# Blockwise decaying attention and a Mish MLP on one core: the head in a new order, and the first two groups' states taken head by head

## The chip, the cores and the metric

The kernel runs on one core of a Trainium2 chip. The metric is the device time of one execution in microseconds (us). The engines are TensorE (PE in the profile, PEld for its weight loads), VectorE (DVE), ScalarE (ACT), GpSimd (POOL) and the queue of SyncE (SP). They run their own instruction streams in order and wait for each other by semaphores.

## What is computed

The reference runs a linear attention with a decay per head over blocks of 64 positions, and then a two-layer MLP on the result:

```python
for b in range(nb):                       # 12 blocks of 64; B, H, S, D = 4, 8, 768, 64
    intra = einsum('bhic,bhjc->bhij', qb, kb) * Dmask      # lam ** (i - j), causal
    intra = einsum('bhij,bhjd->bhid', intra, vb)
    inter = einsum('bhid,bhde->bhie', qb * lam_pow, kv_state)
    out[:, :, sl] = intra + inter
    kv_state = lam_block * kv_state + einsum('bhsd,bhse->bhde', kb * rev_pow, vb)
x = out as (3072, 512)
h = x @ w_in                              # w_in 512 x 2048
g = h * tanh(softplus(h))                 # Mish
result = g @ w_out                        # w_out 2048 x 512
```

## The kernel before

It works in chunks of 128 positions of one batch with all eight heads. Chunk c belongs to group c // 4 (six groups: positions 128 n to 128 n + 127 of the four batches). Heads are paired: JP = 4 pairs j, and t = 0, 1 within a pair.

For the chunks 0 to 7, the first two groups, three steps each do the attention on TensorE: `first_t` (the turn) transposes k and q (8 matmuls into the PSUM tiles `pk` and `pq`; ACT copies the first to `pkT`, DVE the second to `pqT`); `first_s` makes the scores (8 matmuls into two tiles `pS`, then two DVE products `sb` with the decay mask `dm` in group 0 and with a causal mask in group 1); `first_o` makes the outputs (8 matmuls with the values `vz` into `pO`, in group 1 also 4 with the state `wst`; ACT copies `pO` to `xt`, the MLP's input). `vz` is 128 wide for each head, with zeros in its upper half.

The first layer of the MLP for group 0 is 16 units u of four 128x512 matmuls (`mm1_unit`, L399), each followed by Mish on ACT; for group 1 it is 16 tiles of sixteen 128x128 matmuls (`mm1_tile`, L417). Before the last chunk of group 0 is there, `mm1_part` runs units 0, 1 and 2 on the first three chunks (384 columns), and the rest of 128 columns, the tail, follows. The second layer is `mm2_unit` (L431), four 128x512 matmuls each.

The states: `state_step` multiplies a chunk's decayed keys `ktil` (k times `lk`; made by `scale_k`, on DVE for group 0 and on POOL for group 1) with its values, in four 128x128 matmuls per chunk, one for each pair. That gives a pair's two own 64x64 blocks and two cross blocks. In group 0 a product with `lbm` (the block decay in the own blocks, zero elsewhere) writes `wst`. In group 1 the sum with `wst` goes to `raw`, and POOL writes the own blocks times the decay to `wcp`, in two 64x256 products per chunk. From group 2 on `group_state` does without cross blocks: sixteen matmuls for two chunks in 128x64 column tiles (L319), the lower 64 columns for t = 0 and the upper for t = 1.

From group 2 on, `turn` transposes by DMA on SP's queue (`qraw`, `kraw`), `pair_s` makes the scores of two chunks, `pair_o` their outputs, and these stand among the dense units of the group before. The loop of group 2's attention (n = NT - 1 = 1) runs among 32 `mm2_unit`, four for each chunk of groups 0 and 1: `pair_s` after units 9 and 16, `pair_o` after 13 and 20.

What sets the order: everything is written out by hand (`manual_schedule`), so each engine runs in program order. `busy(m)` puts m matmuls of zeros on TensorE. Loads of k, q, v and the weights go through POOL's queue in the order of the code, and `scale_k` of group 1 stands among them. A load that follows eight others waits until the one of the same semaphore has landed. PSUM has 8 banks: `ph` 2, `po` 2, `pS`, `pk`, `pq`, `pO` 1 each.

Of the kernel before, what the change touches and what calls it, by code (L numbers as in the profile page):

```python
# [20 lines left out]
def kernel(  # L21
# [12 lines left out]
    C = 128  # L34
# [117 lines left out]
    nc.vector.memset(one1, 1.0)  # L152
    for i in range(B):
        nc.vector.memset(vz[i][:, :, D : 2 * D], 0.0)
# [13 lines left out]
    busy(3)  # L168

    lnb = const.tile([128, H], F32, name="lnb")  # L170
    nc.scalar.activation(lnb, lamb, AF.Ln)

    dm = const.tile([128, 2, JP, C], F32, name="dm")
    lk = const.tile([128, H], F32, name="lk")
    lnp = const.tile([128, JP], F32, name="lnp")
# [10 lines left out]
    def pair_decays():  # L186
        lnh = lnb.rearrange("p (j t) -> p j t", t=2)
        for hp in range(2):
            rs = slice(64 * hp, 64 * hp + 64)
            nc.vector.tensor_copy(lnp[rs, :], lnh[rs, :, hp])  # L190

    def q_arguments():
        nc.vector.tensor_tensor(out=lq, in0=bc(ei, 1, JP), in1=bc(lnp, 2, C), op=ALU.mult)

    def q_decays():
        nc.scalar.activation(lq, lq, AF.Exp)
# [12 lines left out]
    def first_t(c):  # L209

        out_ = []
        first = c < B
        for src, name in ((k0 if c == 0 else kn[c] if first else ktil[c], "pk"),
                          (q0 if c == 0 else qn[c], "pq")):
            pt = ps.tile([128, JP, C], F16, name=name, tag=name)
            for j in range(JP):
                nc.tensor.matmul(
                    pt[:, j, :], src[:, 2 * j : 2 * j + 2, :].rearrange("p h c -> p (h c)"), ident,
                    is_transpose=True, start=(j == 0), stop=(j == JP - 1),
                )  # L220
# [23 lines left out]
    def first_o(c):  # L244
# [5 lines left out]
        for j in range(JP):  # L250
            if n:
                nc.tensor.matmul(psO[:, j, :], wst[b][j // 2][:, j % 2, :],
                                 kq[c][1][:, j, :], start=True, stop=False)
            for t in range(2):
                o = 4 * D * j + D * t
                nc.tensor.matmul(psO[:, j, :], vf[:, o : o + 128], sb0[c][t][:, j, :],
                                 start=(n == 0 and t == 0), stop=(t == 1))
# [20 lines left out]
    wst = [[const.tile([128, 2, 128], F16, name=f"w{b}{hf}") for hf in range(2)] for b in range(B)]  # L278
# [5 lines left out]
    def state_step(n, b, spare):  # L284

        i = n * B + b
        pv = ps.tile([128, JP, 128], F32, name="pv", tag=spare, bufs=2)
        for j in range(JP):
            nc.tensor.matmul(
                pv[:, j, :].rearrange("p (a e) -> p a e", a=2),  # L290
                ktil[i][:, 2 * j : 2 * j + 2, :].rearrange("p h c -> p (h c)"),
                vz[i % NVB][:, 2 * j : 2 * j + 2, 0:D], start=True, stop=True,
            )
        if n:
            raw = work.tile([128, JP, 128], F32, name="raw", tag="raw", bufs=4)
        for hf in range(2):
            hs = slice(2 * hf, 2 * hf + 2)
            if n == 0:
                nc.vector.tensor_tensor(
                    out=wst[b][hf], in0=pv[:, hs, :], in1=lbm[:, hs, :], op=ALU.mult)  # L300
            else:
                nc.vector.tensor_tensor(
                    out=raw[:, hs, :], in0=pv[:, hs, :], in1=wst[b][hf], op=ALU.add)
        if n:
            for t in range(2):
                rs = slice(64 * t, 64 * t + 64)
                nc.gpsimd.tensor_tensor(
                    out=wcp[b // 2][0][rs, b % 2, :, :], in0=raw[rs, :, rs],
                    in1=bc(lbc[rs, :], 2, D), op=ALU.mult)

    def group_state(n, spare):

        for h in range(2):
            pv = ps.tile([128, 2, JP, D], F32, name="pv", tag=spare, bufs=2)
            for x in range(2):
                i = n * B + 2 * h + x
                for j in range(JP):
                    for t in range(2):
                        nc.tensor.matmul(  # L319
                            pv[64 * t : 64 * t + 64, x, j, :], ktil[i][:, 2 * j + t, :],  # L320
                            vz[i % NVB][:, 2 * j + t, 0:D], start=True, stop=True)
            raw = work.tile([128, 2, JP, D], F32, name="raws", tag="raws", bufs=2)
            nc.vector.tensor_tensor(out=raw, in0=pv, in1=wcp[h][n % 2], op=ALU.add)  # L323
            nc.gpsimd.tensor_tensor(  # L324
                out=wcp[h][(n + 1) % 2], in0=raw, in1=bc(bc(lbc, 1, 2), 3, D), op=ALU.mult)

    def pair_a(s):
        if s.n < NG - 1:
            group_state(s.n, s.spare)
# [63 lines left out]
    def mm1_part(n, ni, lo, hi):  # L393

        if lo == 0:
            ph_t[ni] = ps.tile([128, GT], F32, name="ph",
                               tag="po" if n == 0 and ni == 2 else "ph", bufs=2)
# [85 lines left out]
    nc.scalar.preload_act_table(AF.Mish)  # L483
# [12 lines left out]
    first_s(3)  # L496
# [3 lines left out]
    mm1_part(0, 2, 0, GT - C)  # L500
    scale_k(0)
    nc.vector.memset(lbm, 0.0)
    for hp in range(2):
        rs = slice(64 * hp, 64 * hp + 64)
        nc.vector.tensor_copy(lbm[rs, :, rs], bc(lbc[rs, :], 2, D))
    for i in range(B, NVB - 2):
# [7 lines left out]
    load_q(NVB - 1)  # L514
    load_v(NVB - 1)
    scale_k(B + 2)
# [23 lines left out]
    for f, i in ((load_k, c + 1), (load_q, c + 1), (load_k, c + 2), (load_q, c + 2)):  # L540
        f(i)
    steps = {(4, 0): ((first_o, 5), (first_s, 6)), (4, 1): ((first_t, 7), (state_step, 0)),
             (4, 2): ((first_o, 6), (first_s, 7), (state_step, 1)), (4, 3): ((state_step, 2),),
             (5, 0): ((first_o, 7), (state_step, 3))}
    for c in range(B, 2 * B):
        for s in range(WS):
            mm1_tile(c, s)
            for f, i in steps.get((c, s), ()):
                f(*((1, i, "po") if f is state_step else (i,)))
# [5 lines left out]
    for n in range(NT - 1, NG):  # L555
# [9 lines left out]
        if n + 1 < NG:  # L565
# [5 lines left out]
            steps = (((9, pair_s, 0), (13, pair_o, 0), (16, pair_s, 1), (20, pair_o, 1),  # L571
# [60 lines left out]
```

## Time and profile before

| what | us |
|---|---|
| runs shown (3) | 211.38, 212.17, 212.15; median 212.15 |
| profiled execution, its time | 213.28 |
| its span, first to last instruction | 211.5 |
| TensorE busy / DVE / ACT / POOL | 203.1 / 69.3 / 86.3 / 102.4 |
| ACT's first Mish of group 0 starts | 19.71 |
| first matmul of the second layer | 54.91 |
| last matmul ends, about | 208.4 |

The time is the span and 1.8 us around it. In the profile a row of the timeline has the start, the time from the first start to the last end, the engine, the line, the operation, output <- inputs with their shapes, and in brackets the idle time of the engine before it with what ended that. Rows of the chain of waits have a start, a duration and a name. The state of the DMA engines matters here too: their mean busy share is 90% or more in each of the first 21 of the page's 40 slices.

### The profile page before, as it was taken

The numbers are of one execution on the slowest core, as the hardware profiler recorded it, in microseconds if no ns is written. First come the engines' busy times: TensorE is split into PE (matmuls) and PEld (weight loads), VectorE is DVE, ScalarE is ACT, GpSimd is POOL, SyncE is SP. The second block draws the span as 40 slices with busy tenths as digits, with TensorE's granted clock in tenths as the row PEclk, the third lists the DMA queues.
The fourth block names the chain that finished last, engine by engine and source line by source line (L and its number), as shares of the span: only waits on it lengthen the run. The fifth ranks groups of instructions, "written<-read, shape, count | busy, mean of one in ns | idle before, by whom it ended". The sixth has DMA issues, their size and how long they took to land.

```text
span 211.5 us, 4241 instructions
## 1 busy us (share of the span) xinstructions
PE 203.1 (96%) x1728; PEld 110.2 (52%) x1728; DVE 69.3 (33%) x131; ACT 86.3 (41%) x146; POOL 102.4 (48%) x149
## 2 busy tenths in 40 slices
PE   7798999999997999999999999999999999999994
PEld 2465546999644544455544454544445544444442
DVE  6867746650004442042440042582042600000000
ACT  5664566656321111356412356312456221566120
POOL 7997379948992558796965076931000000000000
PEclk9999999999999999999999999999999999999999
DMA  9999999999999999999996999996902032100112
GB/s 132 132 159 172 192 145 115 152 195 168 114 146 209 195 179 177 171 188 148 149 161 152 190 81 84 144 167 152 183 1 51 3 99 99 51 3 0 50 50 99
DMA packets 109894, 26.76 MB, mean 127 GB/s; under 512 B 102578, under 2 KB 106930, under 8 KB 109874
## 3 DMA queue, kind: packets, MB, share of 16 engines
q0 software_dynamic: 78080, 13.37, 91.8%
q1 hardware_dynamic: 27296, 6.63, 20.4%
q10 hardware_dynamic: 4498, 6.49, 9.9%
q8 instruction: 13, 0.21, 0.5%
q14 instruction: 7, 0.06, 0.1%
HBM read 27.26 MB, written 6.29 MB: 159 GB/s over the span
## 4 chain that ended last, share of the span: by engine, by line
PE 75%; POOL 13%; DMA 9%; issue 1%; DVE 0%; POOLq 0%
PE po L431 35%; PE ph L399 27%; DMA kn<-in_k_dram 6%; PE ph L417 5%; DMA kraw<-ktil 3%; POOL vz L79 3%; POOL ktil L266 3%; POOL qn L76 2%; POOL kn L68 2%; PE pS L343 2%; PE pO L370 2%; POOL win L92 1%; POOL win L95 1%; PE pv L319 1%; PE pO L349 1%
## 5 line engine op out<-in xcount | busy, mean ns | idle before, releaser
L431 PE MATMUL po<-wout,hsg 128*128 128x512 f16 (+2 forms) x400 | 85.4, 371 | 0.0
L399 PE MATMUL ph<-xt,win 128*128 128x512 f16 (+2 forms) x332 | 73.5, 371 | 0.4 <-ACT hsg L406 0.2
L406 ACT ACTIVATE hsg<-ph 128x512 f16<-128x512 f32 x80 | 47.5, 597 | 30.2 <-PE ph L399 29.8
L431 PEld LDWEIGHTS <-hsg 128*128 128x128 f16 x400 | 37.8, 98 | 42.3
L399 PEld LDWEIGHTS <-win 128*128 128x128 f16 x332 | 30.9, 98 | 34.7 <-issue 1.5
L446 ACT ACTIVATE osb<-po 128x512 f32<-128x512 f32 (+1 forms) x24 | 14.2, 593 | 75.4 <-PE po L431 70.6
L358 DVE TENSOR_TENSOR sb<-pS,maskT 128x512 f16<-128x512 f32 x32 | 20.0, 683 | 64.0 <-PE pS L343 64.0
L68 POOL DMA_DIRECT2D kn<-in_k_dram x23 | 20.9, 909 | 5.3 <-issue 1.9
L79 POOL DMA_DIRECT2D vz<-in_v_dram x24 | 21.6, 905 | 2.7 <-DMA win<-in_moe_w_in_dram 2.0
L76 POOL DMA_DIRECT2D qn<-in_q_dram x23 | 20.8, 903 | 3.3 <-DMA wout<-in_moe_w_out_dram 1.9
L266 POOL TENSOR_TENSOR ktil<-kn,lk 128x512 f16<-128x512 f16 x16 | 16.6, 1050 | 3.0 <-ACT hsg L406 2.9
L376 DVE TENSOR_TENSOR xtok<-pO,lqt 128x512 f16<-128x512 f32 x16 | 10.3, 686 | 16.8 <-PE pO L370 16.8
L417 PE MATMUL ph<-xt,win 128*128 128x128 f16 x256 | 15.3, 219 | 0.0
L417 PEld LDWEIGHTS <-win 128*128 128x128 f16 x256 | 14.5, 98 | 0.1
L440 DVE COPY osb<-po 128x128 f32<-128x128 f32 x1 | 0.3, 290 | 38.7 <-PE po L431 38.7
L421 ACT ACTIVATE hsg<-ph 128x512 f16<-128x512 f32 x16 | 9.6, 597 | 6.9 <-PE ph L417 6.9
L387 POOL COPY tick<-hsg 1x1 f16<-1x1 f16 x25 | 4.4, 176 | 12.2 <-ACT hsg L406 12.1
L324 POOL TENSOR_TENSOR wc<-raws,lbc 128x512 f16<-128x512 f32 x6 | 6.6, 1113 | 5.5 <-DVE raws L323 5.5
L163 PE MATMUL busy<-kzero 128*128 128x512 f16 x18 | 7.6, 516 | 1.2 <-DVE kzero L149 1.2
L266 DVE TENSOR_TENSOR ktil<-kn,lk 128x512 f16<-128x512 f16 (+1 forms) x8 | 6.6, 846 | 0.0
L241 DVE TENSOR_TENSOR sb<-pS,maskT 128x512 f16<-128x512 f32 x8 | 5.2, 686 | 4.2 <-PE pS L237 4.2
L343 PE MATMUL pS<-qraw,kraw 64*128 64x128 f16 x128 | 5.1, 218 | 1.2 <-DMA kraw<-ktil 1.2
(72 smaller groups left out, 122.6 us busy)
## 6 DMA issues: line engine op xcount, KB each, us to landing
out_dram<-osb ACTq DMA_DIRECT2D x23, 256.0 KB, 2.6
vz<-in_v_dram POOLq DMA_DIRECT2D x24, 128.0 KB, 4.7
kn<-in_k_dram POOLq DMA_DIRECT2D x23, 128.0 KB, 5.2
qn<-in_q_dram POOLq DMA_DIRECT2D x23, 128.0 KB, 5.0
wout<-in_moe_w_out_dram POOLq DMA_DIRECT2D x4, 512.0 KB, 10.4
win<-in_moe_w_in_dram POOLq DMA_DIRECT2D x3, 512.0 KB, 10.2
kn<-in_k_dram SPq DMA_DIRECT2D x1, 256.0 KB, 3.2
qn<-in_q_dram ACTq DMA_DIRECT2D x1, 256.0 KB, 3.9
```

The source lines that it names most:

```text
L68: nc.gpsimd.dma_start(out=kn[i], in_=chunk_rows(k, i))
L76: nc.gpsimd.dma_start(out=qn[i], in_=chunk_rows(q, i))
L79: nc.gpsimd.dma_start(out=vz[i % NVB][:, :, 0:D], in_=chunk_rows(v, i))
L266: (nc.vector if i < B or i >= (NG - 1) * B else nc.gpsimd).tensor_tensor(out=t, in0=kn[i], in1=bc(lk, 2, D), op=ALU.mult)
L358: nc.vector.tensor_tensor(out=s.sb[x][t], in0=pS[x][t], in1=bc(maskT, 1, JP), op=ALU.mult)
L376: nc.vector.tensor_tensor(out=xtok[:, :, :, t, :], in0=s.pO[t], in1=bc(bc(lqj[:, :, t], 1, 2), 3, D), op=ALU.mult)
L399: nc.tensor.matmul(ph_t[ni][:, lo:hi], win_t(ni, kc), xt[n][:, kc, lo:hi], start=(kc == 0), stop=(kc == NKC - 1))
L406: nc.scalar.activation(hsg[n][:, ni, :], ph_t.pop(ni), AF.Mish)
L417: nc.tensor.matmul(ph[:, u, :], win_t(w * s + u, kc), xt[n][:, kc, b * C : (b + 1) * C], start=(kc == 0), stop=(kc == NKC - 1),)
L421: nc.scalar.activation(hsg[n][:, w * s : w * s + w, b * C : (b + 1) * C], ph, AF.Mish)
L431: nc.tensor.matmul(po[:, lo:hi], hsg[n][:, ki, b * C : (b + 1) * C], wout[part][:, kk, lo:hi], start=(ki == 0), stop=(ki == NKI - 1),)
L446: nc.scalar.activation(o, i, AF.Copy)
```

## The change

The head (group 0's attention) is laid out anew, the decays by pair come from ScalarE, and the states of groups 0 and 1 are made head by head. Cut to what is spoken of:

```diff
+    half = const.tile([1, 2, 128], F32, name="half")
+    nc.vector.memset(half, 0.0)
+    for t in range(2):
+        nc.vector.memset(half[:, t, 64 * t : 64 * t + 64], 1.0)
...
     nc.tensor.matmul(lamb, one1, lam1, start=True, stop=True)
-    busy(3)
+    lamp = ps.tile([128, JP], F32, name="lamp", tag="pS")
+    for t in range(2):
+        nc.tensor.matmul(lamp, half[:, t, :], lam1.rearrange("p (j t) -> p j t", t=2)[:, :, t],
+                         start=(t == 0), stop=(t == 1))
+    busy(1)
...
-    def q_arguments():
-        nc.vector.tensor_tensor(out=lq, in0=bc(ei, 1, JP), in1=bc(lnp, 2, C), op=ALU.mult)
     def q_decays():
-        nc.scalar.activation(lq, lq, AF.Exp)
-        nc.scalar.activation(lqt, lnb, AF.Exp, scale=eq)
-    lbm = const.tile([128, JP, 128], F32, name="lbm")
+        for j in range(JP):
+            nc.scalar.activation(lq[:, j, :], ei, AF.Exp, scale=lnp[:, j : j + 1])
...
-    def first_t(c):
+    def first_t(c, m=0):
...
                 nc.scalar.activation(out_[-1], pt, AF.Copy)
+                busy(m)
...
+    def state_half(n, h, spare, bufs=2):
+        pv = ps.tile([128, 2, JP, D], F32, name="pv", tag=spare, bufs=bufs)
+        for x in range(2):
+            i = n * B + 2 * h + x
+            for j in range(JP):
+                for t in range(2):
+                    nc.tensor.matmul(
+                        pv[64 * t : 64 * t + 64, x, j, :], ktil[i][:, 2 * j + t, :],
+                        vz[i % NVB][:, 2 * j + t, 0:D], start=True, stop=True)
+        rows = [slice(64 * t, 64 * t + 64) for t in range(2)]
+        own = [wst[rs, 2 * h : 2 * h + 2, :, rs] for rs in rows]
+        if n == 0:
+            for rs, o in zip(rows, own):
+                nc.vector.tensor_tensor(
+                    out=o, in0=pv[rs], in1=bc(bc(lbc[rs, :], 1, 2), 3, D), op=ALU.mult)
+            return
+        raw = work.tile([128, 2, JP, D], F32, name="raws", tag="raws", bufs=2)
+        if n == 1:
+            for rs, o in zip(rows, own):
+                nc.vector.tensor_tensor(out=raw[rs], in0=pv[rs], in1=o, op=ALU.add)
+        else:
+            nc.vector.tensor_tensor(out=raw, in0=pv, in1=wcp[h][n % 2], op=ALU.add)
+        nc.gpsimd.tensor_tensor(
+            out=wcp[h][(n + 1) % 2], in0=raw, in1=bc(bc(lbc, 1, 2), 3, D), op=ALU.mult)
...
+    def clear(b):
+        nc.vector.memset(wst[:, b], 0.0)
+
     nc.scalar.activation(k0, kn[0], AF.Copy)
+    nc.scalar.activation(lnp, lamp, AF.Ln)
     decays(0)
-    pair_decays()
+    decays(1)
     nc.vector.tensor_copy(q0, qn[0])
     nc.scalar.activation(dm[:, 0], dm[:, 0], AF.Exp)
-    decays(1)
-    first_t(0)
+    first_t(0, 2)
+    clear(0)
     nc.scalar.activation(dm[:, 1], dm[:, 1], AF.Exp)
-    q_arguments()
+    nc.scalar.activation(lk, lnb, AF.Exp, scale=ek)
+    nc.scalar.activation(lqt, lnb, AF.Exp, scale=eq)
+    nc.scalar.activation(lbc, lnp, AF.Exp, scale=float(C))
     busy(1)
     first_s(0)
-    nc.scalar.activation(lk, lnb, AF.Exp, scale=ek)
-    nc.scalar.activation(lbc, lnp, AF.Exp, scale=float(C))
+    first_t(1)
+    clear(1)
     q_decays()
-    busy(2)
-    first_t(1)
-    nc.scalar.preload_act_table(AF.Mish)
     busy(1)
+    first_o(0)
     first_s(1)
-    first_o(0)
     busy(3)
     first_t(2)
-    busy(1)
+    clear(2)
+    nc.scalar.preload_act_table(AF.Mish)
+    first_o(1)
     first_s(2)
-    first_o(1)
     busy(3)
     first_t(3)
+    clear(3)
+    first_s(3)
     first_o(2)
-    busy(1)
-    first_s(3)
+    busy(2)
     mm1_part(0, 0, 0, GT - C)
     first_o(3)
     mm1_part(0, 1, 0, GT - C)
-    mm1_part(0, 2, 0, GT - C)
     scale_k(0)
-    nc.vector.memset(lbm, 0.0)
-    for hp in range(2):
-        rs = slice(64 * hp, 64 * hp + 64)
-        nc.vector.tensor_copy(lbm[rs, :, rs], bc(lbc[rs, :], 2, D))
+    scale_k(1)
...
+    scale_k(B + 2)
     load_v(NVB - 1)
-    scale_k(B + 2)
...
-    steps = {11: ((first_t, 4),), 13: ((first_s, 4),), 14: ((first_t, 5),),
-             15: ((first_o, 4), (first_s, 5), (first_t, 6))}
+    steps = {12: ((first_t, 4),), 14: ((first_s, 4),), 15: ((first_t, 5), (first_o, 4))}
     for u in range(NKI):
         mm1_unit(0, u)
-        if u in (3, 5, 7, 9):
-            state_step(0, (u - 3) // 2, "po")
-        if u in (1, 3, 5):
-            scale_k((u + 1) // 2)
+        if u in (1, 3):
+            state_half(0, u // 2, "po")
+        if u == 1:
+            scale_k(2)
+            scale_k(3)
...
-    steps = {(4, 0): ((first_o, 5), (first_s, 6)), (4, 1): ((first_t, 7), (state_step, 0)),
-             (4, 2): ((first_o, 6), (first_s, 7), (state_step, 1)), (4, 3): ((state_step, 2),),
-             (5, 0): ((first_o, 7), (state_step, 3))}
+    steps = {(4, 0): ((first_s, 5), (first_t, 6)), (4, 1): ((first_o, 5), (first_s, 6)),
+             (4, 2): ((first_t, 7),), (4, 3): ((first_o, 6), (first_s, 7)), (5, 0): ((first_o, 7),),
+             (6, 1): ((state_half, 0),), (6, 2): ((state_half, 1),)}
...
-            steps = (((9, pair_s, 0), (13, pair_o, 0), (16, pair_s, 1), (20, pair_o, 1),
+            steps = (((11, pair_s, 0), (14, pair_o, 0), (17, pair_s, 1), (20, pair_o, 1),
                       (24, pair_a, 1)) if n < NT else
```

Of the 18 zero matmuls 16 are left, two of them new between the k and the q half of chunk 0's turn. `wst` is now one tile, cleared per chunk by DVE.

ACT, from the copy of chunk 0's k to the second `xt`. Before:

```order
L467 ACTIVATE k_94<-kn_98 128x512
L471 ACTIVATE dm<-dm 128x512
L223 ACTIVATE pkT<-pk 128x512
L474 ACTIVATE dm<-dm 128x512
L478 ACTIVATE lk<-lnb,ek 128x8
L479 ACTIVATE lbc<-lnp 128x4
L196 ACTIVATE lq<-lq 128x512
L197 ACTIVATE lqt<-lnb,eq 128x8
L223 ACTIVATE pkT<-pk 128x512
L483 ACT_TABLE_LOAD
L258 ACTIVATE xt<-pO 128x4x128
```

The same place now, to the second `xt`:

```order
L456 ACTIVATE dm<-dm 128x512
L219 ACTIVATE pkT<-pk 128x512
L459 ACTIVATE dm<-dm 128x512
L460 ACTIVATE lk<-lnb,ek 128x8
L461 ACTIVATE lqt<-lnb,eq 128x8
L462 ACTIVATE lbc<-lnp 128x4
L219 ACTIVATE pkT<-pk 128x512
L196 ACTIVATE lq<-ei,lnp 128x128 x4
L255 ACTIVATE xt<-pO 128x4x128
L219 ACTIVATE pkT<-pk 128x512
L474 ACT_TABLE_LOAD
L255 ACTIVATE xt<-pO 128x4x128
```

The four `lq` stand behind chunk 1's `pkT`, and the table load for Mish has moved back behind chunk 2's `pkT`, ahead of the second `xt` (it was ahead of the first).

DVE, from the last scores of group 0 to the states (`ktil` are the decayed keys of chunks 0 to 3, `w` and `wst` the states). Before:

```order
L241 TENSOR_TENSOR sb<-pS,dm 128x512 x2
L266 TENSOR_TENSOR ktil<-kn_98,lk 128x512
L502 MEMSET lbm 128x512
L505 COPY lbm<-lbc 64x4x64 x2
L266 TENSOR_TENSOR ktil<-kn,lk 128x512
L299 TENSOR_TENSOR w_158<-pv,lbm 128x256
L299 TENSOR_TENSOR w_159<-pv,lbm 128x256
```

The same place now:

```order
L238 TENSOR_TENSOR sb<-pS,dm 128x512 x2
L263 TENSOR_TENSOR ktil<-kn_98,lk 128x512
L263 TENSOR_TENSOR ktil<-kn,lk 128x512
L295 TENSOR_TENSOR wst<-pv,lbc 64x8x64 x2
L263 TENSOR_TENSOR ktil<-kn,lk 128x512 x2
L295 TENSOR_TENSOR wst<-pv,lbc 64x8x64 x2
L515 TENSOR_SCALAR maskT<-rel 128x128
```

Two chunks' keys stand ahead of the first state products, and the keys of chunks 2 and 3 behind them.

POOL, where group 1's state ends and the loads for group 2 go on (`raw` and `raws` are sums from DVE, `kn` and `qn` chunk 11's loads, `ktil` the keys of chunk 8):

```order
 L68 DMA kn<-in_k_dram 128x8x64
 L76 DMA qn<-in_q_dram 128x8x64
-L307 TENSOR_TENSOR wc_166<-raw,lbc 64x256 x4
-L307 TENSOR_TENSOR wc_168<-raw,lbc 64x256 x4
+L304 TENSOR_TENSOR wc_163<-raws,lbc 128x512
+L304 TENSOR_TENSOR wc_165<-raws,lbc 128x512
 L68 DMA kn<-in_k_dram 128x8x64
 L76 DMA qn<-in_q_dram 128x8x64
-L266 TENSOR_TENSOR ktil<-kn,lk 128x512 x2
+L263 TENSOR_TENSOR ktil<-kn,lk 128x512 x2
```

Eight products have become two of the whole partition height, in the same place of POOL's order.

More of the change, by code (lines that the diff above doesn't have):

```diff
@@ L275, in turn @@
             nc.sync.dma_start_transpose(out=to[i], in_=src[i].rearrange("p h c -> p (h c)"))
-    wst = [[const.tile([128, 2, 128], F16, name=f"w{b}{hf}") for hf in range(2)] for b in range(B)]
+    wst = const.tile([128, B, JP, 128], F16, name="wst")
     wcp = [[const.tile([128, 2, JP, D], F16, name=f"wc{h}{r}") for r in range(2)] for h in range(2)]
@@ L282 @@
         pass
[L284 to L322, printed above, removed]
+    def state_half(n, h, spare, bufs=2):
[11 more added lines that the diff above has]
+            for rs, o in zip(rows, own):
+                nc.vector.tensor_tensor(
+                    out=o, in0=pv[rs], in1=bc(bc(lbc[rs, :], 1, 2), 3, D), op=ALU.mult)
[5 more added lines that the diff above has]
+        else:
@@ L323, in group_state @@
             nc.vector.tensor_tensor(out=raw, in0=pv, in1=wcp[h][n % 2], op=ALU.add)
-            nc.gpsimd.tensor_tensor(
-                out=wcp[h][(n + 1) % 2], in0=raw, in1=bc(bc(lbc, 1, 2), 3, D), op=ALU.mult)
+        nc.gpsimd.tensor_tensor(
+            out=wcp[h][(n + 1) % 2], in0=raw, in1=bc(bc(lbc, 1, 2), 3, D), op=ALU.mult)
     def pair_a(s):
         if s.n < NG - 1:
-            group_state(s.n, s.spare)
+            for h in range(2):
+                state_half(s.n, h, s.spare)
@@ L396, in mm1_part @@
             ph_t[ni] = ps.tile([128, GT], F32, name="ph",
-                               tag="po" if n == 0 and ni == 2 else "ph", bufs=2)
+                               tag="ph", bufs=2)
         for kc in range(NKC):
@@ L548 @@
             for f, i in steps.get((c, s), ()):
[L549 removed]
+                f(*((1, i, "po") if f is state_half else (i,)))
     c = 2 * B
```

9 lines of the change are left out of this document (2 added, 7 removed).

## The prediction

> **What bounds the kernel now.** I read the page first, then the chain of waits, then the timeline of the first 75 us, since the change touches little behind that.
>
> ```profile
> PE 203.1 (96%) x1728; PEld 110.2 (52%) x1728; DVE 69.3 (33%) x131; ACT 86.3 (41%) x146; POOL 102.4 (48%) x149
> ```
>
> TensorE is busy nearly always, so a change pays by less matmul work, by an earlier start of the dense work, or by a wait taken out of it. The chain of waits (start, duration, what) says which wait ends last:
>
> ```profile
> 15.22 12.64 DMA kn<-in_k_dram
> ...
> 34.50 1.08 POOL ktil L266
> ...
> 35.62 0.40 PE pk L217 x4
> 36.02 0.22 PE pq L217 x4
> ...
> 37.81 0.33 PE pS L237 x8
> ...
> 39.58 0.22 PE pv L289 x4
> ...
> 58.47 6.72 DMA kraw<-ktil
> ...
> 65.23 0.40 PE pS L343 x8
> 65.63 0.23 PE pO L349 x16
> ...
> 69.89 2.59 PE po L431 x12
> ...
> 72.48 0.55 PE pS L343 x16
> ...
> 80.74 0.62 PE pv L319 x32
> ```
>
> Up to 35.6 it is POOL's loads and `ktil`; then TensorE follows itself, except for one DMA, chunk 9's transposed keys, which land at 65.2. Behind that all is TensorE. So two stretches count: from the head to the second layer's start at 54.91, and from there through `pair_s`. The last rows give prices: 0.216 for a dense 512-column matmul (2.59 / 12), so 0.865 for a unit of four; 0.22 for a chunk's old state; 0.31 for half a new one (0.62 / 2); 0.78 for a `pair_s` that waits for nothing (0.55 + 0.23).
>
> **The head.** Rows of the timeline, with start and duration:
>
> ```profile
> 3.42 1.14 DVE L182 SCALAR_TENSOR_TENSOR dm<-rel,lnb,gone 128x128 f32<-128x128 f32 x4 [0.39 <-ACT lnb L171]
> ...
> 7.91 0.63 ACT L196 ACTIVATE lq<-lq 128x512 f32<-128x512 f32 x1
> 8.02 1.29 DVE L241 TENSOR_TENSOR sb<-pS,dm 128x512 f16<-128x512 f32 x2
> ...
> 9.55 0.63 PE L163 MATMUL busy<-kzero 128*128 128x512 f16 x1
> ...
> 9.98 1.28 ACT L483 ACT_TABLE_LOAD   x1
> ...
> 11.40 0.81 PE L163 MATMUL busy<-kzero 128*128 128x512 f16 x3
> ...
> 16.25 1.29 DVE L241 TENSOR_TENSOR sb<-pS,dm 128x512 f16<-128x512 f32 x2 [0.56 <-PE pS L237]
> ...
> 18.18 0.60 ACT L258 ACTIVATE xt<-pO 128x512 f16<-128x512 f32 x1 [1.88 <-PE pO L256]
> ...
> 19.87 0.69 DVE L266 TENSOR_TENSOR ktil<-kn,lk 128x512 f16<-128x512 f16 x1
> ...
> 21.45 1.90 PE L399 MATMUL ph<-xt,win 128*128 128x512 f16 x8
> 21.64 0.75 DVE L299 TENSOR_TENSOR w<-pv,lbm 128x256 f16<-128x256 f32 x2 [1.08 <-PE pv L289]
> ```
>
> The reader sees a loop on DVE: two `sb` of 0.645 each, then the next chunk's `pqT` and scores, then `sb` again. I replay the new order with such durations; a cold matmul of 512 columns takes 0.63 with its latency, a warm one less (three in 0.81).
>
> Chunk 0: q's cast now stands behind all eight decay rows, at 3.42 + 2 x 1.14 = 5.7, so `sb` starts at about 8.2 (was 8.02). Chunk 1: its scores now stand behind `first_o(0)`, which needs the second `sb` of chunk 0 (9.5); with eight matmuls at the cold rate `sb` starts at 10.9, as before. Chunk 2: its turn no longer follows outputs, `sb` 13.2, 0.4 earlier than before. Chunk 3: on ACT, chunk 2's `pkT` ends at 12.65, the table load (1.28) at 13.93, the second `xt` (0.60) at 14.53, chunk 3's `pkT` at 15.13; scores, then `sb` 15.6 to 16.9, 0.6 earlier (was 16.25 to 17.54). But `first_o(2)` and its `xt` now follow these scores (`xt` ends at 16.7), and unit 0's first part, 0.65, stands ahead of `first_o(3)`: the last `xt` runs 18.04 to 18.64, where it ran 18.18 to 18.78. Of 0.6 there is 0.14 left. Two tails and the first half state follow on TensorE, to about 19.6.
>
> Now the new wait. DVE makes two state products, 19.8 to 21.1, and only then the keys of chunks 2 and 3, at 0.69 each, to 22.45. TensorE is through unit 3 at about 21.5 and comes to the second half state, which needs these keys: it waits 0.9. Unit 4 starts at about 22.65 instead of 21.45: **+1.2**. It could not have started much before 21.45 anyhow: its weights, issued at 13.03 (the start of the three in the first row), take 8.4 to land (the second row, from the view of DMA issues there), so 21.4.
>
> ```profile
> 13.03 2.32 POOL L95 DMA_DIRECT2D win<-in_moe_w_in_dram  x3
> ```
> ```profile
> win<-in_moe_w_in_dram POOLq DMA_DIRECT2D x1, 512.0 KB, 8.4
> ```
>
> What I cost at nothing here: the sum by halves for `lnp` (two matmuls like `lamb`, done by 4.3, under k's copy, which ends at 4.60); three small memsets, 0.5 at most, ahead of the identity, which is needed at 4.65; four clears of 0.27 under the scores that DVE waits for. The four `lq` are not in the trace at 128 columns: between 0.29 (the 128x8 rows of ACT) and 0.63 (512 columns) each, 1.1 to 2.5 in all; ACT's slot ends at 12.05 and opens at 9.35, so both ends fit; were it longer, it would delay chunk 2's `pkT` one to one. The state product of 64x512 is not there either: 0.42 by the 128x256 product (half its columns), 1.04 by twice this copy:
>
> ```profile
> L505 DVE COPY lbm<-lbc 64x256 f32<-64x256 f32 x2 | 1.0, 522 | 0.1
> ```
>
> I take `sb`'s 0.645, the nearest in columns and source; the ends move unit 4 by -0.45 and +0.8.
>
> **From unit 4 to the second layer.**
>
> ```profile
> 36.08 1.06 PE L417 MATMUL ph<-xt,win 128*128 128x128 f16 x16
> ...
> 47.61 5.41 POOL L307 TENSOR_TENSOR wc<-raw,lbc 64x256 f16<-64x256 f32 x8
> ...
> 54.91 7.29 PE L431 MATMUL po<-wout,hsg 128*128 128x512 f16 x33
> ```
>
> The stretch was 54.91 - 21.45 = 33.46. In it stood seven old states, 7 x 0.22 = 1.55; now two halves stand there, 0.62 and some 0.1 for being apart: **-0.8**. The rest of the work is the same. Waits: before about 1.45 (33.46 less the work), above all for POOL's `ktil` of chunks 4 to 6. These go, since TensorE now comes later than the keys. What is late next is ACT. From unit 4 at 22.65, nine units end at 30.45, chunk 4's turn (0.45, the two rows from 35.62 on) at 30.9, two units at 32.6, its scores (0.33) at 32.95, unit 15 at 33.8, chunk 5's turn at 34.25, chunk 4's outputs at 35.0. Between these and the first tile stands nothing any more, and `xt` (0.60) queues behind a Mish and a `pkT` of as much each, 34.1 to 35.3: it ends at 35.9, a wait of 0.9. Four more on DVE's `sb` and `pqT` add 0.8. That is 1.75: **+0.3**. The second layer starts at 54.91 + 1.2 - 0.8 + 0.3 = 55.6.
>
> Here the Trainium skill speaks against the change: in "TensorEngine Tiling (Array Packing)", Restrictions, column tiling is said to disable Fast Weight Load. The row agrees that a load takes longer (112 ns for half the columns, against 98 ns):
>
> ```profile
> L289 PEld LDWEIGHTS <-ktil 128*128 128x128 f16 x32 | 2.3, 98 | 1.3 <-issue 0.3
> ...
> L319 PEld LDWEIGHTS <-ktil 128*64 128x64 f16 x96 | 1.8, 112 | 1.3 <-issue 1.3
> ```
>
> Were none of it hidden, an estimate by that page is 64 x 0.112 = 7.2 in place of the seven times 0.22 of this stretch and one ahead of it (1.8), a loss of 5.4; the 0.62 for 32 such matmuls in the chain decides against it.
>
> **Through `pair_s`.**
>
> ```profile
> 63.64 0.40 PE L343 MATMUL pS<-qraw,kraw 64*128 64x128 f16 x8
> ...
> 65.23 0.40 PE L343 MATMUL pS<-qraw,kraw 64*128 64x128 f16 x8 [1.19 <-DMA kraw<-ktil]
> ...
> 65.79 3.63 PE L431 MATMUL po<-wout,hsg 128*128 128x512 f16 x16
> ```
>
> After ten units `pair_s` took 63.64 to 65.79, 2.15 instead of 0.78: 1.37 of waiting. Now twelve units stand ahead of it, and it comes at 55.6 + 10.4 = 66.0. Will chunk 9's keys be there? POOL's eight products (47.61 to 53.02) become two:
>
> ```profile
> L324 POOL TENSOR_TENSOR wc<-raws,lbc 128x512 f16<-128x512 f32 x6 | 6.6, 1113 | 5.5 <-DVE raws L323 5.5
> ```
>
> But their sums come from the half states after tiles (6, 1) and (6, 2), at 51.3 for the last on TensorE, 52.65 on DVE, so POOL ends at 53.75, 0.7 later than 53.02. Behind it queue chunk 11's loads, `ktil` of chunks 8 to 11, the value loads, and on SP the transposes: the keys land at 65.2 + 0.7 = 65.9, where TensorE wants them at 66.2. The wait goes with a margin of 0.3: **-1.4**. The second `pair_s` comes 6.4 behind the first, at 72.4, as before (72.48).
>
> **Sum:** +1.2 - 0.8 + 0.3 - 1.4 = -0.7. Everything later moves with TensorE. The profiled execution took 213.28 (span 211.5 and 1.8 around it), 1.1 more than the median of the runs shown, 212.15. The sum would make it 212.6, and the median 211.4, which I predict.
>
> **Rivals.**
>
> *The clock warms earlier.* In the rows of `busy`, TensorE is slow until about 11.1 (0.63 at 9.55, three in 0.81 at 11.40). If two zero matmuls in chunk 0's turn warm it before 9.5, `first_o(0)` and chunk 1's scores shorten by 0.45, the zeros behind by up to 0.6; ACT's and DVE's path moves by 0.7 up to unit 4 (21.9), and the rest with it: 211.4 - 0.7 = 210.7. For it: less idle from 4.6 to 7.7 (0.8, was 1.6). Against it: the stretch from 1.2 to 4.6 had little idle and did not do it. The Trainium skill, "TensorE: Matmul & The Clock Gate", Part 1, has the clock gate judged in free-running windows of 3.4 us: counted back from 11.1 that is 7.7 for this rival; a longer time is not shown by any row here.
>
> *The state products are cheap (0.42).* Two of them end 0.45 earlier, and with them unit 4 and all behind it: 211.4 - 0.45 = 210.9; with some of the later waits on DVE gone too, 210.7. For it: the trace has no product over half the partitions. Against it: every DVE product of 512 columns in it takes 0.64 to 0.69, whatever its source.
>
> *The wait stays.* Keys 9 are later than 66.2 by as much as they now take in vain: 0.3 to 0.8 lost, 211.7 to 212.2. For it: a margin of 0.3 on a landing of 6.72. Then the change does not do what it says for `pair_s`.
>
> *Slower: loads overtake the keys of chunk 11.*
>
> ```profile
> HBM read 27.26 MB, written 6.29 MB: 159 GB/s over the span
> ```
> ```profile
> 64.98 1.37 SPq L275 DMA_TRANSPOSE kraw<-ktil  x1
> ```
> ```profile
> kraw<-ktil SPq DMA_TRANSPOSE x1, 6.7
> ```
>
> Two loads, of chunk 13, follow unit 11, which now ends ahead of the first `pair_s` instead of behind it, so they are issued some 2.5 earlier against the transposes. A load reads 0.262 MB (128 x 512 x 4 bytes), 1.65 us at that rate. Chunk 11's keys, issued at 64.98, took 6.7 to land (the view of DMA issues around it): 71.7. If both loads get ahead of them, they land at 75.0 against a need at 72.4: 2.6 of waiting, 211.4 + 2.6 = 214.0. The kernel is slower than before from a landing 0.7 behind the need. For it: the second `pair_s` comes no later than it did, and the keys start 0.7 later on SP. Against it: loads and transposes go through queues of their own, and in the 58.47 row the keys landed with loads beside them.
>
> **Chances.** Forecast 0.43 (own range 210.9 to 211.9), clock 0.18, cheap products 0.11, the wait stays 0.17, slower 0.11. About 0.5% (1.06 us) is what a measurement here can tell from no change. Faster is below 211.1: the second and third case and a quarter of the forecast, 0.4. Slower is above 213.2: most of the last case, 0.09. The rest is 0.51. The range, 210.2 to 212.9, leaves out the last case and the far ends of the fast ones.
>
> **What would show it.** In the new profile: the last `xt` of the head ends at about 18.6; DVE's `ktil` of chunks 2 and 3 end near 22.4, and a wait of TensorE for them; unit 4 at 22.65; a wait of ACT's `xt` ahead of the first tile near 35 to 36; the second layer at 55.6; no wait for `kraw` at 66. It would be wrong with a second layer before 55 (clock or product), or with a `pS` row that waits for `kraw`.

## The result, and the profile after

| | us |
|---|---|
| before, seven runs | 210.88 to 212.17, median 211.54 |
| after, seven runs | 212.38 to 213.88, median 213.74 |
| ratio | 1.009 (95%: 1.0063 to 1.0117) |
| profiled execution: before, after | 213.28, 213.85 |

The change makes the kernel 0.9% slower. The forecast was 211.4, so it is 2.3 too low, and the time lies outside its range. (The median of before is 211.54 over seven runs; the three that the forecast could use had 212.15.) The two profiled executions differ by 0.6 only. That is the first clue: the one of after is like its timed runs (0.1 above their median), and the one of before is 1.7 above its own.

The view of waits (engine, line, what it waited for: us in total, times, longest) of after, the rows on which TensorE loses time that the change moved:

```profile
PE pS L324 <- DMA kraw<-ktil: 1.1, 2, 0.6
PE ph L398 <- ACT xt L255: 0.7, 1, 0.7
...
PE pv L288 <- DVE ktil L263: 0.6, 2, 0.3
```

The reader sees two waits for transposed keys where the prediction had taken one away, and the two it had foreseen: ACT's `xt` ahead of the first tile, DVE's `ktil` at the second half state. The timeline of after around unit 4, TensorE, and then DVE:

```profile
18.76 0.44 PE L288 MATMUL pv<-vz,ktil 128*64 128x64 f16 x16
19.29 1.89 PE L380 MATMUL ph<-xt,win 128*128 128x512 f16 x8
21.48 0.32 PE L288 MATMUL pv<-vz,ktil 128*64 128x64 f16 x8 [0.30 <-DVE ktil L263]
22.09 0.32 PE L288 MATMUL pv<-vz,ktil 128*64 128x64 f16 x8 [0.29 <-DVE ktil L263]
22.33 1.90 PE L380 MATMUL ph<-xt,win 128*128 128x512 f16 x8
```
```profile
19.31 1.39 DVE L295 TENSOR_TENSOR wst<-pv,lbc 64x512 f16<-64x512 f32 x2 [1.75 <-ACT hsg L387]
20.74 1.29 DVE L263 TENSOR_TENSOR ktil<-kn,lk 128x512 f16<-128x512 f16 x2
```

Unit 4 starts at 22.33, because DVE makes the keys of chunks 2 and 3 behind the two state products. The second layer and the scores of the pairs:

```profile
55.44 0.81 PE L412 MATMUL po<-wout,hsg 128*128 128x512 f16 x3
65.90 0.62 PE L324 MATMUL pS<-qraw,kraw 64*128 64x128 f16 x16
72.44 0.40 PE L324 MATMUL pS<-qraw,kraw 64*128 64x128 f16 x8
73.40 0.40 PE L324 MATMUL pS<-qraw,kraw 64*128 64x128 f16 x8 [0.56 <-DMA kraw<-ktil]
91.86 0.40 PE L324 MATMUL pS<-qraw,kraw 64*128 64x128 f16 x8
92.75 0.40 PE L324 MATMUL pS<-qraw,kraw 64*128 64x128 f16 x8 [0.49 <-DMA kraw<-ktil]
```

The first `pair_s` (65.90) no longer waits. The second waits for chunk 11's keys and the first one of group 3 for chunk 13's. Where the keys come from is seen on POOL, in after and then in before:

```profile
46.32 0.88 POOL L76 DMA_DIRECT2D qn<-in_q_dram  x1 [3.04 <-DMA wout<-in_moe_w_out_dram]
51.25 1.04 POOL L304 TENSOR_TENSOR wc<-raws,lbc 128x512 f16<-128x512 f32 x1 [4.05 <-DVE raws L301]
52.60 1.04 POOL L304 TENSOR_TENSOR wc<-raws,lbc 128x512 f16<-128x512 f32 x1 [0.31 <-DVE raws L301]
53.58 0.94 POOL L68 DMA_DIRECT2D kn<-in_k_dram  x1
```
```profile
46.72 0.87 POOL L76 DMA_DIRECT2D qn<-in_q_dram  x1 [1.91 <-DMA wout<-in_moe_w_out_dram]
47.61 5.41 POOL L307 TENSOR_TENSOR wc<-raw,lbc 64x256 f16<-64x256 f32 x8
```

In before POOL goes on as soon as the weights land; its eight products are long, but nothing of TensorE holds them up. In after POOL stands idle for 4.05 ahead of the first of its two short products, until TensorE has come to the half states behind tiles (6, 1) and (6, 2). In these two profiles the products end only 0.6 apart, at 53.0 and 53.6. Everything behind them in POOL's program (chunk 11's loads, the keys of chunks 8 to 11, and through SP their transposes) now hangs on TensorE's own progress.

### The profile page after: what moved, and what is told of

Its sections match the earlier page's. It is cut to its first block, busy times and chain, and to the rows that moved or that the text cites. A ratio compares the mean times of both kernels' runs of the same rounds, so it can differ in the third digit from the quotient of the medians.

```text
span 212.1 us, 4293 instructions
## 1 busy us (share of the span) xinstructions
PE 203.5 (96%) x1758; PEld 110.5 (52%) x1758; DVE 67.6 (32%) x124; ACT 86.7 (41%) x150; POOL 100.0 (47%) x143
## 4 chain that ended last, share of the span: by engine, by line
PE 82%; DMA 9%; DVE 2%; ACT 1%; POOL 1%; issue 1%; SPq 1%; POOLq 0%; ACTq 0%; DVEq 0%
PE po L412 33%; PE ph L380 30%; DMA kraw<-ktil 7%; PE ph L398 7%; PE pO L253 2%; PE pS L324 2%; DMA kn<-in_k_dram 2%; PE pO L351 2%; PE pS L234 1%; PE pv L288 1%; PE pk L213 1%; SPq L272 1%; PE busy L167 1%; PE pq L213 1%; POOL vz L79 1%
## 5 line engine op out<-in xcount | busy, mean ns | idle before, releaser
L304 POOL TENSOR_TENSOR wc<-raws,lbc 128x512 f16<-128x512 f32 x8 | 8.6, 1096 | 9.8 <-DVE raws L303 5.4
L167 PE MATMUL busy<-kzero 128*128 128x512 f16 x16 | 6.6, 505 | 1.2 <-DVE kzero L149 1.2
L253 PE MATMUL pO<-sb,vz 128*128 128x128 f16 x64 | 6.4, 230 | 0.4 <-DVE sb L238 0.3
```

## The experiments

Each profiled execution can be cut at the second layer's start, S. This table has S, the wait in `pS` rows for transposed keys, and the span less S:

| profiled execution | S | wait for keys | span - S |
|---|---|---|---|
| before | 54.91 | 1.2 | 156.6 |
| after | 55.44 | 1.1 | 156.7 |
| before, once more (e1) | 55.41 | 0.3 | 156.0 |
| after, old places (e2) | 54.97 | 1.2 | 156.8 |
| before, new places (e3) | 54.69 | none | 155.2 |
| after, keys first (e4) | 54.24 | 0.8 | 156.2 |
| after, states early (e5) | 55.95 | none | 155.2 |
| e4 and e5 (e6) | 54.23 | none | 155.2 |
| e6 and cover for xt (e7) | 54.11 | none | 155.2 |
| before, states late (e8) | 53.90 | 0.9 | 156.3 |
| e7, table later (e9) | 54.24 | none | 155.3 |
| after, chunk 13's loads later (e10) | 54.99 | 2.3 | 157.7 |
| e7, old places (e11) | 54.10 | none | 155.2 |
| after, chunk 12's loads later (e12) | 54.95 | none | 155.2 |

From S on, every one of them takes 155.2 to 155.3 without a wait for keys, and with one the wait and 0.2 to 0.5 more. So a time is made of S, 155.2, that wait with what comes beside it, and the 1.8 around the span. Both kernels' second half is the same, and only two things are left to explain.

**e1: the kernel before, once more.** No edit.

> The kernel before, unchanged, profiled once more. Theory L (landing by chance): the wait of 1.2 us for chunk 9's keys at the first pair_s belongs to the one profiled execution of 213.28 us and not to the timed ones (median 211.5), so a second profile shows under 0.4 us of it and a time near 211.7. Rival P (the wait is regular): the second profile again shows 1 us or more of it, and its time is again 1 us or more above the timed ones.

Measured: 211.91, ratio 1.0007 (0.9978 to 1.0037); the profiled execution took 213.16. Each theory misses in one half: the wait for keys is small this time, as L said, but the execution is as long as P said, for another reason. The waits:

```profile
PE ph L399 <- DMA win<-in_moe_w_in_dram: 1.5, 1, 1.5
...
PE pS L343 <- DMA kraw<-ktil: 0.3, 1, 0.3
```

Here unit 2's weights landed late. A wait of a microsecond for a transfer comes and goes from one execution of this program to the next.

**e2: after, with the old places.**

```diff
-            steps = (((11, pair_s, 0), (14, pair_o, 0), (17, pair_s, 1), (20, pair_o, 1),
+            steps = (((9, pair_s, 0), (13, pair_o, 0), (16, pair_s, 1), (20, pair_o, 1),
```

> The changed kernel with pair_s and pair_o back behind units 9, 13, 16 and 20. Theory of the place (the move itself costs, by loads of chunk 13 that go out earlier and so delay the keys of chunks 11 and 13): the waits for both keys go, 1.1 us less than the changed kernel, about 212.6. Theory of the head (the second layer starts 0.5 later and the sums reach POOL later, so keys are late wherever pair_s stands): TensorE comes to the first pair_s at 64.1 and waits about 1 us for keys that land at 65.2; within 0.4 of the changed kernel, 213.4 to 214.1.

Measured: 213.54, ratio 1.0085 (1.0057 to 1.0113), the same as after. The wait is back at the first `pair_s`, about as long as the two it replaces (1.05 together):

```profile
65.32 0.40 PE L324 MATMUL pS<-qraw,kraw 64*128 64x128 f16 x8 [1.22 <-DMA kraw<-ktil]
```

So the move of the pairs is not what costs. The keys are late wherever the pairs stand, and the move only chooses which of them TensorE waits for.

**e3: before, with the new places.** The same line, the other way round.

> The kernel before with pair_s and pair_o behind units 11, 14, 17 and 20 and nothing else changed. Prediction as it stands on record: 1.4 us gained by the keys' wait, 210.1. Theory L: that wait is not there in timed runs, so nothing is gained: 211.3 to 211.9. Theory of the place: waits for the keys of chunks 11 and 13 come, 1.1 us slower, 212.6.

Measured: 211.91, ratio 0.9995 (0.9963 to 1.0027). The move gains nothing, where the prediction had put its largest term, 1.4. In its profile there is no wait for keys:

```profile
65.14 0.62 PE L343 MATMUL pS<-qraw,kraw 64*128 64x128 f16 x16
```

But POOL shows that the old place would hardly have had one either:

```profile
45.53 5.42 POOL L307 TENSOR_TENSOR wc<-raw,lbc 64x256 f16<-64x256 f32 x8
```

Up to this row the program is that of before, and the row stands 2.1 earlier than 47.61, because the weights ahead of it landed earlier. Chunk 9's keys landed at about 62.6 (issued at 56.40, 6.2 to land) instead of 65.2, against a need at about 64.

**e4: after, with the keys of chunks 2 and 3 ahead of the state products.**

```diff
-    scale_k(0)
-    scale_k(1)
+    for i in range(B):
+        scale_k(i)
...
-        if u == 1:
-            scale_k(2)
-            scale_k(3)
```

> The changed kernel with DVE making the keys of chunks 2 and 3 right behind those of chunks 0 and 1, ahead of the first state products. Theory of DVE's order: the two waits of 0.3 us for these keys at the second half state go, unit 4 starts at 21.6 to 21.8 instead of 22.33 and all behind it 0.6 earlier: second layer at 54.9, 213.1. Rival: the stretch is refilled by the next wait (the weights of unit 4, or ACT's xt ahead of the first tile), and under 0.2 is gained: 213.6.

Measured: 212.43, ratio 1.0034 (1.0011 to 1.0057): by the ratios 0.56% or 1.2 us better than after, twice the 0.6 expected, though the two intervals leave room for some 0.4 to 1.9. TensorE, in e2 and then in e4:

```profile
21.62 0.32 PE L288 MATMUL pv<-vz,ktil 128*64 128x64 f16 x8 [0.29 <-DVE ktil L263]
21.86 2.33 PE L380 MATMUL ph<-xt,win 128*128 128x512 f16 x10
```
```profile
18.83 1.89 PE L380 MATMUL ph<-xt,win 128*128 128x512 f16 x8
20.65 0.44 PE L288 MATMUL pv<-vz,ktil 128*64 128x64 f16 x16
21.13 3.63 PE L380 MATMUL ph<-xt,win 128*128 128x512 f16 x16
```

The half state no longer waits. Unit 4 starts 0.73 earlier than in e2 (21.13 against 21.86), whose head is otherwise timed like this one, and no wait for weights takes the place. In the profiles some more is gained after S, where the keys' wait was 0.8 here against 1.2 in e2 and 1.1 in after; how much of that the timed runs have is not shown.

**e5: after, with group 1's half states four tiles earlier.**

```diff
-             (6, 1): ((state_half, 0),), (6, 2): ((state_half, 1),)}
+             (5, 1): ((state_half, 0),), (5, 2): ((state_half, 1),)}
```

> The changed kernel with group 1's half states behind tiles (5, 1) and (5, 2) instead of (6, 1) and (6, 2). Theory of POOL's queue: the loads of chunk 11, the keys of chunks 8 to 11 and their transposes stand behind POOL's two products, which now end at about 50.9 instead of 53.64; keys 9 and 11 land 2 us or more earlier, the waits of 1.1 us at pair_s go, 212.6. Rival: the landing is set by the transfers themselves (transposes that take 5 to 8 us among other loads), not by when POOL issues them; the waits stay, 213.4 to 213.9.

Measured: 212.2, ratio 1.003 (1.0011 to 1.0048). POOL, and the two `pair_s`:

```profile
48.18 1.04 POOL L304 TENSOR_TENSOR wc<-raws,lbc 128x512 f16<-128x512 f32 x1 [2.06 <-DVE raws L301]
49.53 1.04 POOL L304 TENSOR_TENSOR wc<-raws,lbc 128x512 f16<-128x512 f32 x1 [0.31 <-DVE raws L301]
```
```profile
66.41 0.62 PE L324 MATMUL pS<-qraw,kraw 64*128 64x128 f16 x16
...
72.95 0.62 PE L324 MATMUL pS<-qraw,kraw 64*128 64x128 f16 x16
...
91.62 0.62 PE L324 MATMUL pS<-qraw,kraw 64*128 64x128 f16 x16
```

POOL is through 3 us sooner (50.6 instead of 53.6), and all the waits for keys are gone, those of group 3 too. With no other edit this takes back 0.6% (1.3 us) of the 0.9% lost. Chunk 11's keys now landed in 4.8 from their issue; in after it was 8.5 (the views of DMA issues there):

```profile
kraw<-ktil SPq DMA_TRANSPOSE x1, 4.8
```
```profile
kraw<-ktil SPq DMA_TRANSPOSE x1, 8.5
```

**e6: both edits.**

> Both edits of the two runs before: keys of chunks 2 and 3 first, and group 1's half states behind tiles (5, 1) and (5, 2). If the two causes add, the first's 1.3 us and the second's 1.1 us are gained against the changed kernel: 211.3 to 211.6, level with the kernel before. If keys first already took out what the keys' waits cost in timed runs, it stays near 212.4.

Measured: 211.46, ratio 0.9983 (0.9966 to 1.0). The two causes together make up the whole loss: by the ratios 1.07% or 2.3 us against after, where each alone gave 1.2 and 1.3, so they add within what these intervals tell. S is 54.23 here and 54.24 in e4, so moving the half states changed nothing ahead of the second layer: what e5's edit gains lies behind S, where the waits for keys were.

**e7: chunk 5's scores behind unit 15 as well.**

```diff
-    steps = {12: ((first_t, 4),), 14: ((first_s, 4),), 15: ((first_t, 5), (first_o, 4))}
+    steps = {12: ((first_t, 4),), 14: ((first_s, 4),), 15: ((first_t, 5), (first_o, 4), (first_s, 5))}
...
-    steps = {(4, 0): ((first_s, 5), (first_t, 6)), (4, 1): ((first_o, 5), (first_s, 6)),
+    steps = {(4, 0): ((first_t, 6),), (4, 1): ((first_o, 5), (first_s, 6)),
```

> The run with both edits, and chunk 5's scores behind unit 15 (after chunk 4's outputs) instead of behind tile (4, 0). Theory of the missing cover: TensorE does these scores (0.33 us) while ACT makes the xt that the first tile waits for (0.69 us), so the wait falls to about 0.35 and all behind it comes 0.33 earlier: 0.3 less than without this edit. Rival: the 0.33 is given back at a later wait (DVE's sb, or keys): no difference over 0.1.

Measured: 211.26, ratio 0.9989 (0.9966 to 1.0013). The wait for `xt` falls from 0.69 in e6 to 0.18, further than the 0.35 expected:

```profile
34.35 1.05 PE L398 MATMUL ph<-xt,win 128*128 128x128 f16 x16 [0.69 <-ACT xt L255]
```
```profile
34.66 1.05 PE L398 MATMUL ph<-xt,win 128*128 128x128 f16 x16 [0.18 <-ACT xt L255]
```

S is only 0.12 earlier than in e6 (54.11), since unit 4 waited 0.22 for its weights in this execution and the head was 0.13 later before that. The time is 0.2 below e6, which these intervals do not tell from nothing.

**e8: before, with its states late.**

```diff
-    steps = {(4, 0): ((first_o, 5), (first_s, 6)), (4, 1): ((first_t, 7), (state_step, 0)),
-             (4, 2): ((first_o, 6), (first_s, 7), (state_step, 1)), (4, 3): ((state_step, 2),),
-             (5, 0): ((first_o, 7), (state_step, 3))}
+    steps = {(4, 0): ((first_o, 5), (first_s, 6)), (4, 1): ((first_t, 7),),
+             (4, 2): ((first_o, 6), (first_s, 7)), (5, 0): ((first_o, 7),),
+             (5, 3): ((state_step, 0),), (6, 0): ((state_step, 1),), (6, 1): ((state_step, 2),),
+             (6, 2): ((state_step, 3),)}
```

> The kernel before with its four state steps of group 1 behind tiles (5, 3) to (6, 2) instead of (4, 1) to (5, 0); no other edit. Theory of POOL's queue: POOL's eight products end at about 54.4 instead of 51 to 53, keys 9 land near 66.5 against a need at 64.2, and TensorE waits about 2 us at the first pair_s: 213.3 to 214. Rival (the place of the states does not matter to the keys): 211.5 to 212.

Measured: 212.45, ratio 1.0039 (1.0004 to 1.0074). The direction is the expected one, the size half of it, and just clear of none. POOL's products ended at 52.6 rather than 54.4, since TensorE was early in this execution (S at 53.90) and the sums held their start up by 0.38 only:

```profile
47.19 5.39 POOL L307 TENSOR_TENSOR wc<-raw,lbc 64x256 f16<-64x256 f32 x8 [0.38 <-DVE raw L302]
```

So this run bears only weakly on the cause: the products ended no later than in the profile of before (53.0), and the 0.38 does not account for the whole wait of 0.9 for keys.

**e9: e7 with ACT's table load behind chunk 3's turn.**

```diff
     clear(2)
-    nc.scalar.preload_act_table(AF.Mish)
...
     first_t(3)
+    nc.scalar.preload_act_table(AF.Mish)
     clear(3)
```

> The run with three edits (keys first, states early, chunk 5's scores behind unit 15), and ACT's table load of 1.28 us behind chunk 3's turn instead of chunk 2's. Theory of the head: chunk 3's pkT no longer queues behind the table load, the wait of 0.67 us ahead of chunk 3's scores goes, unit 4 comes 0.5 earlier and so does the end: 210.8. Rival (the weights' landing bounds unit 4, near 21.1 to 21.4 in the rows of before): a wait for the weights takes the place of the one removed, under 0.2 gained: 211.1 to 211.4.

Measured: 211.24, ratio 0.9977 (0.9949 to 1.0006), the same as e7. The rival holds: the wait for chunk 3's `pkT` falls only from 0.67 to 0.53, and the waits for ACT's `xt` (0.25 in e7) and for the weights of unit 4 (0.22) grow.

```profile
15.93 0.81 PE L380 MATMUL ph<-xt,win 128*128 128x384 f16 x4 [0.52 <-ACT xt L255]
...
21.57 2.76 PE L380 MATMUL ph<-xt,win 128*128 128x512 f16 x12 [0.37 <-DMA win<-in_moe_w_in_dram]
```

**e10: after, with chunk 13's loads later.** This is the slower rival on record.

```diff
-                    u = 7 + x // 2 * 4
+                    u = (7, 15, 15, 19, 23, 27)[x // 2]
```

> The changed kernel with the loads of chunk 13's keys and queries behind unit 15 instead of unit 11, nothing else. Theory of overtaking (the slower rival on record: chunk 13's loads, issued ahead of their old place against the transposes, delay chunk 11's keys): chunk 11's keys land 1.5 to 2.5 us earlier, the second pair_s does not wait, 212.6 to 213.2. Theory of POOL's queue (the keys start late because of the half states): chunk 11's keys land within 0.7 us of 73.35, the waits stay at about 1 us, 213.5 to 214.

Measured: 214.41, ratio 1.0131 (1.0091 to 1.0172). It is slower, and no load of chunk 13 was issued before 71.55. Yet chunk 11's keys took 8.0 to land, and landed even later than in after:

```profile
74.65 0.40 PE L324 MATMUL pS<-qraw,kraw 64*128 64x128 f16 x8 [2.26 <-DMA kraw<-ktil]
```

So these loads do not overtake the keys; that rival's cause is refuted. SP itself was later: it issued them at 66.62, where after has 64.83. Two transposes ahead held its queue for 2.3 and 2.5 instead of 1.2:

```profile
56.05 2.29 SPq L272 DMA_TRANSPOSE kraw<-ktil  x1
...
64.07 2.45 SPq L272 DMA_TRANSPOSE qraw<-qn  x1
66.62 1.66 SPq L272 DMA_TRANSPOSE kraw<-ktil  x1
```

Why the timed runs of e10 are slower than after (by 0.7) I did not find out.

**e11: e7 with the old places.** The line of e2.

> The run with three edits, and pair_s and pair_o back behind units 9, 13, 16 and 20. With keys 9 landing near 62 and keys 11 near 70, theory L says that no place makes TensorE wait: within 0.3 of the run with three edits, 211.0 to 211.6. If the later place is worth something of its own (sums and copies better covered), 0.5 or more slower: 211.8.

Measured: 211.25, ratio 0.9969 (0.9946 to 0.9992), the same as e7. Once the keys are early, the place of the pairs is worth nothing either way. By its ratio this version is 0.3% faster than the kernel before and 1.2% faster than the change. It is the only one whose interval stays below 1, but e7 and e9 are not told from it.

**e12: after, with chunk 12's loads later** (behind unit 11 instead of 7, and chunk 13's behind 15, as in e10).

```diff
-                    u = 7 + x // 2 * 4
+                    u = (11, 15, 15, 19, 23, 27)[x // 2]
```

> The changed kernel with the loads of chunk 12 behind unit 11 instead of 7, and those of chunk 13 behind 15 instead of 11. Chunk 11's keys took 8.5 us to land in the changed kernel and 4.8 with the states early, where chunk 12's loads were issued behind the last transpose instead of ahead of it. Theory of overtaking by chunk 12's loads: chunk 11's keys now land in 5 to 6.5 us, at 70.5 to 72, the second pair_s does not wait, and 0.6 to 1.4 us are gained: 212.3 to 213.2. Theory of POOL's queue alone (they start late, and other traffic such as the value loads fills the time): they land at 73 or later as before, 213.5 to 214.4.

Measured: 213.25, ratio 1.0062 (1.0033 to 1.0091), spread from 211.95 to 214.25. In the profiled execution the keys landed in 5.4, at 70.8, with no wait. But this execution is the fastest of its twelve, and the median lies only 0.5 below that of after, which the intervals do not tell from nothing. Whether chunk 12's loads have a share in the long landing stays open. For it: in e5 and e12 alone both loads went out behind the transpose of chunk 11's keys, and these landed in 4.8 and 5.4, where the other twelve profiles have 5.8 to 8.7. Against it as the whole cause: in e6, e7 and e9 both loads went ahead, and the keys still landed in 6.5, 6.2 and 5.8, with no wait.

## Why the prediction was wrong, point by point

**The head was read right, its sizes a little off.** The last `xt` ended at 18.17 (18.6 forecast), the keys of chunks 2 and 3 at 22.03 (22.4), unit 4 started at 22.33 (22.65). The unknown state product took 0.69, near the 0.645 chosen; the four `lq` took 0.39 each, inside their bounds. The waits came where they were said to come; those at the second half state were 0.59 together, where 0.9 was forecast. Against the 21.45 of before, unit 4 came 0.9 later, not 1.2, and e4 shows that DVE's order alone costs 0.7.

**From unit 4 to the second layer** the stretch was 33.11 (55.44 - 22.33) against 32.95 forecast. The half states of group 1 cost TensorE 0.37 each (49.22 to 49.59, say), as the 0.31 and 0.05 in the sum; the loss of 5.4 that weight loads in column tiles might have meant did not come. The waits of this stretch were misread on both sides, and the errors cancel. TensorE's idle time in it is 0.55 in before and 0.95 in after (0.69 for `xt`, 0.26 for DVE's `sb`), where the sum has 1.45 and 1.75: POOL's `ktil` cost 0.3 before, not most of 1.45, and of the four waits on DVE that were to add 0.8 one of 0.26 came. The difference, +0.4, is close to the +0.3 of the sum. S was 55.44, forecast 55.6.

**"The wait goes with a margin of 0.3: -1.4" is the step that failed**, in two ways. In the profile of after the wait at the first `pair_s` did go: chunk 9's keys landed at 65.2, ahead of their need. But that was worth nothing in the timed runs, and other waits came.

First, the wait it removes is a property of one execution, not of the kernel. Three profiles of the same program up to that point have it at 1.2, 0.3 and, by the landing, none (before, e1, e3), and e3, which makes this move alone, gains nothing. How many timed executions of before have it stays unknown, since only the profiled ones can be looked into. The prediction then counted it twice: it subtracted 1.4 from the profiled 213.28, and afterwards 1.1 more to get from that execution to the median, as if the two had nothing to do with each other. After's own profile lies 0.1 from its median.

Second, "the second `pair_s` comes at 72.4, as before" took it that keys 11 would be in time, as before. The same paragraph carries POOL's lateness of 0.7 through to chunk 9's keys, and stops. Carried on to chunk 11's it would have given 71.7 + 0.7 = 72.4, still ahead of the second half of the scores, which could start at 72.84. So the term that failed is the landing, which was taken as fixed. SP issued these keys no later than in the profile of before (64.83 against 64.98), but they took 8.5 to land instead of 6.7:

```profile
64.83 2.39 SPq L272 DMA_TRANSPOSE kraw<-ktil  x1
```

That the place of the half states decides whether they are in time is shown by e5 (1.3 in the timed runs). All profiles agree: with the half states late (after, e2, e4, e10, e12) keys 11 landed at 70.8 to 74.6; with them early (e5, e6, e7, e9, e11) at 67.8 to 69.8, because SP issued them at 62.3 to 63.6 instead of 63.7 to 66.6 and because most landed sooner, in 4.8 to 6.9 instead of 5.4 to 8.7. Why the transfer itself takes longer in the late group stays open.

The wait of 0.49 for chunk 13's keys in after is not explained by this. POOL began to make them as early as in before (82.89 and 82.99), SP issued them 1.2 later (86.37 against 85.21), and e2, e4, e10 and e12, with the same half states, have no such wait.

Together: on the scale of the profiles the sum said 212.6 and after took 213.85, 1.25 more, which is 1.1 of waits for keys and 0.4 of small losses beside them (156.7 against 155.2), with S 0.2 early. The step to the median, 1.1, should not have been taken. That is the 2.3 missed.

**The rivals.** "The wait stays" happened in another place, and larger. The slower rival named the right keys, chunk 11's, with the wrong cause: e10 refutes the overtaking by chunk 13's loads. "The clock warms earlier" seems to have happened, in part, in some executions. e2, which has the same head as after, ran chunk 1's second transposes in 0.39, after in 0.63 (e2, then after):

```profile
4.74 0.61 PE L213 MATMUL pk<-ident,k 128*128 128x128 f16 x4 [0.18 <-ACT lnp L452]
...
8.05 0.39 PE L213 MATMUL pq<-ident,qn 128*128 128x128 f16 x4
```
```profile
4.85 0.61 PE L213 MATMUL pk<-ident,k 128*128 128x128 f16 x4 [0.29 <-ACT lnp L452]
...
8.19 0.63 PE L213 MATMUL pq<-ident,qn 128*128 128x128 f16 x4
```

The first half state came at 18.30 in e2 and at 18.76 in after. Of these 0.46, 0.11 was there before, at chunk 0's first transposes (4.74 against 4.85), so faster matmuls made at most 0.35, not the 0.7 of the rival, and it differs between executions of one head. The granted clock reads 1.00 from 8 to 9 in both profiles, so that the clock is the reason is inferred from the durations alone. The Trainium skill, "TensorE: Matmul & The Clock Gate", Part 1, says that the window is free-running and the count of cold matmuls changes between runs of one kernel; the two rows of 0.39 and 0.63 fit that.

## What to carry to other kernels

Before a wait for a transfer is put into a sum as a gain, look whether the profiled execution is slower than the timed ones by about as much; if so, it may not be there in most runs, a second profile is worth having, and the same time must not come off twice. A margin of some tenths on a transfer that lands anywhere from 4.8 to 8.7 after its issue, in programs that differ little, is a chance, not a term of a sum. When a producer's queue is tied to the consumer's progress (here POOL's products to late half states), follow everything behind it in that queue to its last consumer, not only to the next one. Work that others queue behind should be placed as early as its inputs allow, even where the engine that does it has time to spare.

## What the runs showed of the hardware that I had not expected

A transpose by DMA of one chunk (128 x 512, two bytes) held SP's queue for 1.2 to 2.5 in programs that differ little; chunk 11's keys landed 4.8 (e5) to 8.7 (e4) after their issue. The weights ahead of POOL's products let these start at 45.53 in one execution and at 47.61 in another with the same program up to there. The same four matmuls of the head took 0.39 in one execution and 0.63 in another, with a granted clock of 1.00 in both profiles.
